# Attention and mixture of experts on one core: sums of squares in bfloat16, and the last scatter behind a branch

## The chip, the core and the metric

The kernel runs as one program on one core of a Trainium2 chip. Its time is the device time in microseconds (us) of one execution; where several runs were made, the median is given. The engines are named as the profile names them: PE is TensorE (PEld its weight loads), DVE is VectorE, ACT is ScalarE, POOL is GpSimd and SP is SyncE, which here issues most of the DMAs. A letter q behind a name (POOLq) marks instructions of the engine's sequencer: branches, semaphore waits, loads of a register.

## The reference

Attention of two kinds is added and goes, as 4608 rows of 512 numbers, into a mixture of eight experts, of which each row takes the likeliest one.

```python
# q, k, v: 8 batches x 8 heads x 576 x 64, float32
out_d = sm_attn(mean of 4 rows of q, of k, of v)        # 144 x 144, then repeated 4 times
mask = np.abs(pos[:, None] - pos[None, :]) < 4
attn = softmax(where(mask, 0.125 * q @ k.T, -1e9))
x = (repeat(out_d, 4) + attn @ v)                       # -> x: 4608 x 512

N, D, E, F = (4608, 512, 8, 1024)
logits = normed(x) @ normed(expert_emb).T / tau
expert_idx = np.argmax(logits, axis=1)
gate_w = softmax(logits)[arange(N), expert_idx]
for e in range(E):
    mask = expert_idx == e
    h = np.maximum(x[mask] @ w1[e], 0.0)                # 512 -> 1024
    out[mask] = gate_w[mask, None] * (h @ w2[e])        # 1024 -> 512
```

All inputs and the output are float32.

## The kernel before

**Stages.** Attention runs first (32 units of a batch and two heads, until about 335 us); its rows go to DRAM (`xd`) and are sorted by expert. The experts' part works in slots of 128 rows that all have one expert: an expert's rows are padded to whole slots, so their number depends on the data. Up to 43 + 3 slots are written out: 3 early ones, which take rows of the first six batches, 38 fixed ones (`NFIX`), which always run, and up to 5 further ones (`last_slots`), which stand in a branch on a flag (`flg`) that the routing writes. With these inputs the flag is zero: 41 slots run, and the further ones don't.

**One slot.** `gather` fetches 128 rows of x by an indirect DMA on POOL (L1091). They are split into two float16 parts and turned. `mm1` multiplies them by the expert's first weights, which lie as two float16 parts `w1h` and `w1l` too: 96 products of 128x128 by 128x128, three to each block (L1170 to L1172). ACT and DVE make the hidden rows from them (L1181, L1182), again as two parts `hT`. `mm2_part` of the slot before multiplies by the second weights, 24 products with 512 columns (L1193 to L1195). `out_rows` scales by the gate `gt` into a tile `o` of two buffers (ACT, L1202), and `store` scatters its 128 rows to their places in the output by an indirect DMA on POOL (L1206). `scale_gate` (POOL, L1157) makes `gt`.

**The weights' scale.** The float16 parts need a power of two near the weights' size. For it each weight matrix that arrives in `st` is squared and summed along its rows by ACT (`square`, L840) into a column of `wsq` (128x2: one column for the first weights, one for the second). In every fixed slot but the last, `total` adds `wsq` over the 128 partitions by a product with a matrix of ones (PE, L848), and DVE takes the result from the bank (L849); `scales` makes the scale and its inverse from the exponent (DVE, L856 and L858). `renew` then decides, by flags of the slot, whether the next slot has a new expert: if so, `split_all` splits the weights (ACT L864, DVE L865, in four pieces), if not, `measure` squares the next ones that have arrived. `measure_now`, in a branch of its own for weights that weren't measured in time, doesn't run with these inputs (no row of L992 in the trace).

**What sets the order.** The whole order is written by hand (`manual_schedule`): each engine's instructions stand in the program in the order in which the code issues them, and tiles with their number of buffers set the waits. Where `renew` branches, each engine concerned takes the branch for itself; the side that isn't taken ends with instructions that bring the semaphores to where the other side would have left them.

**The end.** After the last fixed slot come its second product, `out_rows` and `store`. Then `last_slots` loads the flag into a register on every engine (L1075), and every engine branches (L1076). Where the flag is zero, each engine brings its semaphores up; POOL does it for the eight semaphores of the software DMAs (those that POOL issues) too, with six semaphore instructions and one INC_SWDGE_SEM. Then the program ends (L1334): SP waits for all semaphores, every engine drains, and POOL clears the semaphores.

Of the kernel before, what the change touches and what calls it, by code (L numbers as in the profile page):

```python
# [8 lines left out]
F32 = mybir.dt.float32  # L9
F16 = mybir.dt.float16  # L10
BF16 = mybir.dt.bfloat16
I32 = mybir.dt.int32
AF = mybir.ActivationFunctionType
ALU = mybir.AluOpType
AX = mybir.AxisListType
# [5 lines left out]
N, DM, E, FF = B * S, H * D, 8, 1024  # L21
# [9 lines left out]
SLOT = 128  # L31
NSLOT = N // SLOT + E - 1
NEARLY, BEARLY = 3, B - 2
AHEAD = 4
NFIX = NSLOT - 5
# [14 lines left out]
class Kern:  # L50
# [761 lines left out]
    def weight_tiles(self):  # L812
        w = self.wp = self.pool(self.ctx, "weights", 1)
        self.w1h = w.tile([128, self.KC, FF], F16, name="w1h")
        self.w1l = w.tile([128, self.KC, FF], F16, name="w1l")
        self.w2h = w.tile([128, self.FC, DM], F16, name="w2h")
        self.w2l = w.tile([128, self.FC, DM], F16, name="w2l")
        self.wss = [w.tile([128, NP], F32, name=f"wss{j}") for j in range(2)]
        self.jk = w.tile([128, FF * self.KC // NP], BF16, name="junk")
        self.wmx = w.tile([128, 2], F32, name="wmx")  # L820
        self.wsq = w.tile([128, 2], F32, name="wsq")
        self.wk2 = w.tile([128, 2], I32, name="wk2")
        self.winv = w.tile([128, 2], F32, name="winv")
        self.wscl = w.tile([128, 2], F32, name="wscl")
        self.wold = w.tile([128, 1], F32, name="wold")
        self.wout = w.tile([128, 1], F32, name="wout")
# [6 lines left out]
        n, k = FF // 2, 2 * self.KC // NP  # L833
        return t[:, p % 2 * k:(p % 2 + 1) * k, p // 2 * n:(p // 2 + 1) * n]

    def square(self, src, which, p):

        junk = self.jk[:, :src.shape[1] * src.shape[2]].rearrange("p (c f) -> p c f", c=src.shape[1])
        acc = self.wsq[:, which:which + 1] if p is None else self.wss[which][:, p:p + 1]
        self.nc.scalar.activation(out=junk, in_=src, func=AF.Square, accum_out=acc)  # L840

    def pieces_sum(self, which):
        self.nc.vector.reduce_sum(out=self.wsq[:, which:which + 1], in_=self.wss[which], axis=AX.X)

    def total(self, c):

        ps = self.bank()[:, :c.stop - c.start]
        self.nc.tensor.matmul(out=ps, lhsT=self.onesf, rhs=self.wsq[:, c], start=True, stop=True)  # L848
        self.nc.vector.tensor_scalar(out=self.wmx[:, c], in0=ps, scalar1=1e-36, scalar2=None, op0=ALU.max)  # L849

    def scales(self, c):
# [21 lines left out]
    def first_weights(self):  # L873
# [25 lines left out]
        for p in range(NP):  # L899
            tiles.append(get(0, p))  # L900
            yield FREE
        yield LIGHT
        square(0, 0, 1)
        yield LIGHT
        square(0, 2, 3)
        yield FREE
        self.total(slice(0, 1))
# [9 lines left out]
        split(0, 3)  # L917
        yield LIGHT
        square(1, 0, 1)
        yield LIGHT  # L920
        square(1, 2, 3)
# [66 lines left out]
    def measure_now(self, which):  # L988

        g, c = self.nc.gpsimd, slice(which, which + 1)  # L990
        self.measure(which)
        g.partition_all_reduce(self.wmx[:, c], self.wsq[:, c], channels=128, reduce_op=bass.bass_isa.ReduceOp.add)  # L992
        g.tensor_scalar(out=self.wmx[:, c], in0=self.wmx[:, c], scalar1=1e-36, scalar2=None, op0=ALU.max)
        self.scales(c)

# [27 lines left out]
    def run_slots(self, q0, q1):  # L1023

        last = q1 - 1
        for q in range(q0, q1):
            b = q - NEARLY
            if b + 2 < q1 - NEARLY:
                self.flags(b + 2)
            if q + 2 < q1:  # L1030
                self.x_split(q + 2)
            self.mm1(q)
            if not b:
                self.mm2_part(q - 1, 6, ps=self.begun)
            if q < last:
                self.rescale()
                self.renew(0, b + 1)
                self.stage_next(0, b + 1)
            if not b:
                self.out_rows(q - 1, self.begun)  # L1040
                self.store(q - 1)
            if q + 4 < q1:
                self.gather(q + 4)
            if q < last:
                self.norms(q + 1)
            if q + 3 < q1:
                self.x_size(q + 3)
            self.logits(q)
            if q > q0:
                ps = self.mm2_part(q - 1)  # L1050
                if q < last:
                    self.out_rows(q - 1, ps)
            if q > q0:
                self.renew(1, b)
                if q == last:
                    self.out_rows(q - 1, ps)
                self.stage_next(1, b)
            self.gate(q)
            if q > q0:
                self.store(q - 1)  # L1060
            self.scale_gate(q)
        self.mm2(last)
        self.store(last)

    def open_slots(self, q):

# [131 lines left out]

    def out_rows(self, q, ps):
        s = self.sl[q]  # L1200
        o = s["o"] = self.mg.tile([SLOT, DM], F32, name="o", bufs=2)
        self.nc.scalar.activation(out=o, in_=ps, func=AF.Copy, scale=s["gt"])  # L1202

    def store(self, q):
# [5 lines left out]
    def run(self):  # L1210
        tc, ctx = self.tc, self.ctx
        ctx.enter_context(tc.manual_schedule())
        self.bk = self.pool(ctx, "banks", 7, space=PSUM)
        self.inv = self.pool(ctx, "inverses", 1, space=PSUM).tile([128, 2, G + 4], F32, name="inv")
        self.cp = self.pool(ctx, "const", 1)
        self.dr = self.pool(ctx, "scratch", 1, space=DRAM)
        self.weight_tiles()
        self.slot_pools()
        n = B * NHP
        with ExitStack() as actx:  # L1220
            w0 = self.first_weights()
            steps = self.attention(actx)
            early, heavy = self.early_slots(), FREE
            for at in steps:
                if at is None:
                    break
                if at in EARLY:
                    next(early)
                i, end = at
                if end and i >= 1 and i % NHP in heavy:  # L1230
                    heavy = next(w0, ())

            ps = self.begun
            self.x_size(2)
            self.mm1_half(0, 0, 2, 3, ps[0])
            next(steps)
            self.mm1_half(0, 0, 3, 4, ps[0])
            ps.append(self.mm1_half(0, 1, 0, 2))
            next(steps)
            next(steps)  # L1240
            for _ in steps:
                pass
        self.hd = self.pool(ctx, "hidden", 2)
        self.hidden(0, 0, ps[0])
        self.x_split(2)
        self.mm1_half(0, 1, 2, 4, ps[1])
        self.hidden(0, 1, ps[1])
        self.sw = self.pool(ctx, "slots", 1)
        slots = self.slots()
        next(slots)  # L1250
        w1 = self.second_weights()
        next(w1)
        self.norms(1)
        self.norms(2)
        for _ in range(2):
            next(w1)
        next(slots)
        self.mm1(1)
        ps = self.mm2_part(0, 0, 4)
        next(slots)  # L1260
        for q in range(AHEAD):
            self.gather(NEARLY + q)
        self.mm2_part(0, 4, ps=ps)
        for _ in range(2):
            next(w1)
        self.gates(0)
        self.out_rows(0, ps)
        flags = self.slot_flags()
        next(flags)
        next(slots)  # L1270
        self.hidden(2, 0, self.mm1_half(2, 0))
        self.store(0)
        self.x_T(NEARLY)
        self.hidden(2, 1, self.mm1_half(2, 1))
        next(flags)
        self.norms(NEARLY)
        for _ in range(4):
            next(w1)
        self.gates(1)
        ps = self.mm2_part(1)  # L1280
        next(slots)
        self.out_rows(1, ps)
        self.begun = self.mm2_part(2, 0, 6)
        self.store(1)
        self.x_T(NEARLY + 1)
        for _ in w1:
            pass
        self.gates(2)
        self.x_size(NEARLY + 2)
        self.flags(1)  # L1290
        self.run_slots(NEARLY, NEARLY + NFIX)
        self.last_slots()


@with_exitstack
# [42 lines left out]
```

## Time and profile before

| | |
|---|---|
| time, three runs | 758.92, 760.79 (median), 761.32 us |
| the profiled execution's own time | 763.65 us |
| its span, from the first to the last instruction | 761.9 us |
| PE busy | 715.3 us, 94% of the span |
| DVE, ACT, POOL busy | 464.5, 468.3, 398.8 us |
| attention, to 335 us: PE busy | 304.51 us |
| slots, 342 to 748 us | PE busy 403.7 of 406 us, granted clock 1.00 |
| from 748 us to the end | no matmul |

In a row of a group stand the line, the engine, the operation, output<-inputs, the shape and the count; then the busy time in us and the mean of one in ns; then the time for which the engine stood idle just before, and what ended it. In a row of a stretch each engine has its busy time and count, then come the granted TensorE clock (1.00 is full), the share of the DMA engines and their GB/s. A matmul's record is longer than the distance to the next one's start, since matmuls are pipelined.

### The profile page before, as it was taken

Reading aid. Unit: us, or ns where it says so; the run is one execution under the profiler, and the core shown is the slowest. Engines: PE = TensorE matmul, PEld = TensorE weight load, DVE = VectorE, ACT = ScalarE, POOL = GpSimd, SP = SyncE. Lnnn points to the kernel's source line nnn. Section 1 sums busy time; section 2 is a strip of 40 time slices with the busy share of each in tenths; the row PEclk is TensorE's granted clock in tenths of the full one; section 3 lists DMA queues with packets and bytes.
Section 4 is the critical chain, followed back from the end, with each engine's and each line's share of the span. In section 5 each row is a group of like instructions: output and inputs, shape, how many; then the busy total and the mean of one; then the engine's idle time right before and its main releaser. Section 6 shows DMA issues by size and latency. Waiting matters only on the chain. (4 is left out here: it accounts for less than half of the span.)

```text
span 761.9 us, 27560 instructions
## 1 busy us (share of the span) xinstructions
PE 715.3 (94%) x10540; PEld 542.1 (71%) x10540; DVE 464.5 (61%) x1395; ACT 468.3 (61%) x1095; POOL 398.8 (52%) x800
## 2 busy tenths in 40 slices
PE   7899799999988988999999999999999999999992
PEld 4678587777767767767776777677777777777760
DVE  6577578777778975866636656464654365456320
ACT  4577767778777844465755857676673367357420
POOL 7544455684586653737554555536455444535411
PEclk9999989989999967999999999999999999999997
DMA  9999999999999944735755637378584356338200
GB/s 164 162 206 211 186 205 163 247 160 236 175 198 201 152 162 100 211 78 164 183 98 166 185 113 239 80 213 155 175 181 86 84 155 174 85 125 199 61 27 19
DMA packets 191239, 117.82 MB, mean 155 GB/s; under 512 B 162898, under 2 KB 162898, under 8 KB 191072
## 3 DMA queue, kind: packets, MB, share of 16 engines
q1 hardware_dynamic: 183264, 94.61, 59.1%
q0 software_dynamic: 6560, 19.03, 7.9%
q10 hardware_dynamic: 1248, 2.11, 0.9%
q8 instruction: 85, 1.39, 0.8%
q14 instruction: 82, 0.67, 0.3%
HBM read 213.12 MB, written 20.33 MB: 306 GB/s over the span
## 5 line engine op out<-in xcount | busy, mean ns | idle before, releaser
L1172 PE MATMUL bank<-xT,w1l 128*128 128x128 f16 x1312 | 223.7, 220 | 1.9 <-DVEq L1013 0.8
L1171 PE MATMUL bank<-xT,w1h 128*128 128x128 f16 x1312 | 223.7, 220 | 0.3 <-issue 0.3
L1170 PE MATMUL bank<-xT,w1h 128*128 128x128 f16 x1312 | 223.7, 220 | 0.0
L1170 PEld LDWEIGHTS <-w1h 128*128 128x128 f16 x1312 | 128.8, 98 | 6.1 <-issue 2.0
L1171 PEld LDWEIGHTS <-w1h 128*128 128x128 f16 x1312 | 128.7, 98 | 4.3 <-issue 0.5
L1172 PEld LDWEIGHTS <-w1l 128*128 128x128 f16 x1312 | 128.8, 98 | 3.1 <-DVE w1l L865 2.0
L1195 PE MATMUL bank<-w2h,hT 128*128 128x512 f16 x328 | 124.3, 379 | 0.0
L1194 PE MATMUL bank<-w2l,hT 128*128 128x512 f16 x328 | 124.2, 379 | 0.0
L1193 PE MATMUL bank<-w2h,hT 128*128 128x512 f16 x328 | 124.2, 379 | 0.0
L1206 POOL DMA_INDIRECT out_dram<-o,ids x41 | 53.5, 1305 | 124.1 <-ACTq L1008 82.3
L1182 DVE SCALAR_TENSOR_TENSOR hT<-bank,hT 128x512 f16<-128x512 f32 x82 | 54.9, 686 | 46.0 <-ACT hT L1181 20.1
L390 POOL TENSOR_TENSOR pool_v<-ld_v 72x256 f32<-72x256 f32 x64 | 46.7, 750 | 64.2 <-DMA ld_v<-in_v_dram 48.9
L1181 ACT ACTIVATE hT<-bank 128x512 f16<-128x512 f32 x82 | 46.7, 587 | 52.7 <-PE bank L1172 38.3
L840 ACT ACTIVATE junk<-st 128x1024 bf16<-128x1024 f32 (+1 forms) x30 | 67.5, 2249 | 2.3 <-POOL at L602 1.5
L1121 DVE SCALAR_TENSOR_TENSOR x<-xg,sc,x 128x512 f16<-128x512 f32 x41 | 30.8, 751 | 60.7 <-ACT x L1118 55.2
L1091 POOL DMA_INDIRECT xg<-xd,ids x41 | 44.3, 1080 | 38.5 <-POOLq L1014 17.0
L381 POOL TENSOR_TENSOR pool_kq<-kq 128x288 f32<-128x288 f32 x62 | 43.6, 723 | 34.5 <-ACT kq L368 32.6
L472 ACT ACTIVATE aT<-bank 70x384 f32<-70x384 f32 x96 | 40.0, 484 | 34.0 <-PE bank L469 33.9
L1195 PEld LDWEIGHTS <-hT 128*128 128x128 f16 x328 | 32.0, 98 | 38.8
L1193 PEld LDWEIGHTS <-hT 128*128 128x128 f16 x328 | 35.0, 107 | 33.8
L1194 PEld LDWEIGHTS <-hT 128*128 128x128 f16 x328 | 32.0, 97 | 33.8
L1139 ACT ACTIVATE lg<-lg,lmx 128x8 f32<-128x8 f32 x41 | 12.3, 300 | 67.2 <-DVE lmx L1137 67.2
(236 smaller groups left out, 1547.6 us busy)
## 6 DMA issues: line engine op xcount, KB each, us to landing
st<-in_moe_w_dram SPq DMA_DIRECT2D x148, 1024.0 KB
ld_k<-in_k_dram SPq DMA_DIRECT2D x64, 144.0 KB
ld_q<-in_q_dram SPq DMA_DIRECT2D x64, 144.0 KB
ld_v<-in_v_dram SPq DMA_DIRECT2D x16, 576.0 KB
vw<-in_v_dram SPq DMA_DIRECT2D x16, 576.0 KB
xd<-xr SPq DMA_DIRECT2D x8, 1040.0 KB
st<-in_moe_w_dram SPq DMA_DIRECT2D x12, 512.0 KB
st<-in_moe_w_dram ACTq DMA_DIRECT2D x4, 512.0 KB
```

Of the source, the lines that this page charges most:

```text
L390: g.tensor_tensor(out=t6[:, h], in0=vr[:, :, 0:2 * D], in1=vr[:, :, 2 * D:], op=ALU.add)
L840: self.nc.scalar.activation(out=junk, in_=src, func=AF.Square, accum_out=acc)
L1091: nc.gpsimd.indirect_dma_start(out=xg, out_offset=None, in_=self.xd[:n], in_offset=bass.IndirectOffsetOnAxis(ap=self.ids[:, q:q + 1], axis=0),
L1170: nc.tensor.matmul(out=o, lhsT=self.w1h[:, k, f], rhs=xT[:, 0, k], start=(k == 0), stop=False)
L1171: nc.tensor.matmul(out=o, lhsT=self.w1h[:, k, f], rhs=xT[:, 1, k], start=False, stop=False)
L1172: nc.tensor.matmul(out=o, lhsT=self.w1l[:, k, f], rhs=xT[:, 0, k], start=False, stop=(k == self.KC - 1))
L1181: nc.scalar.activation(out=h[:, 0], in_=ps, func=AF.Relu)
L1182: nc.vector.scalar_tensor_tensor(out=h[:, 1], in0=ps, scalar=0.0, in1=h[:, 0], op0=ALU.max, op1=ALU.subtract)
L1193: nc.tensor.matmul(out=ps, lhsT=hh, rhs=self.w2h[:, j, :], start=(j == 0), stop=False)
L1194: nc.tensor.matmul(out=ps, lhsT=hh, rhs=self.w2l[:, j, :], start=False, stop=False)
L1195: nc.tensor.matmul(out=ps, lhsT=hl, rhs=self.w2h[:, j, :], start=False, stop=(j == self.FC - 1))
L1206: nc.gpsimd.indirect_dma_start(out=self.out, out_offset=bass.IndirectOffsetOnAxis(ap=self.ids[:, q:q + 1], axis=0), in_=o, in_offset=None, ...
```

## The change

There are two edits.

1. `wsq` is kept in bfloat16, and `total` multiplies it by bfloat16 ones (`onesb`, which the routing uses too) in place of float32 ones (`onesf`). `square` and `pieces_sum` write bfloat16; the sum that leads to it is still made in float32 by the engine that writes it. `measure_now` squares into a float32 tile of its own (`wsqf`), since POOL's sum over the partitions reads that, and copies it to `wsq`.
2. `run_slots` doesn't store its last slot any more, unless it is the last of the further ones. The last fixed slot's `store` is called behind `last_slots`, and its rows lie in a tile of their own, `oend`.

```diff
-        self.wsq = w.tile([128, 2], F32, name="wsq")
+        self.wsq = w.tile([128, 2], BF16, name="wsq")
+        self.wsqf = w.tile([128, 2], F32, name="wsqf")
...
-    def square(self, src, which, p):
+    def square(self, src, which, p, acc=None):
...
-        acc = self.wsq[:, which:which + 1] if p is None else self.wss[which][:, p:p + 1]
-        self.nc.scalar.activation(out=junk, in_=src, func=AF.Square, accum_out=acc)
+        if acc is None:
+            acc = self.wsq[:, which:which + 1] if p is None else self.wss[which][:, p:p + 1]
+        with self.nc.allow_low_precision(reason="an exponent is all that is taken of it"):
+            self.nc.scalar.activation(out=junk, in_=src, func=AF.Square, accum_out=acc)
...
     def total(self, c):
...
-        self.nc.tensor.matmul(out=ps, lhsT=self.onesf, rhs=self.wsq[:, c], start=True, stop=True)
+        self.nc.tensor.matmul(out=ps, lhsT=self.onesb, rhs=self.wsq[:, c], start=True, stop=True)
...
     def measure_now(self, which):
...
-        self.measure(which)
-        g.partition_all_reduce(self.wmx[:, c], self.wsq[:, c], channels=128, reduce_op=bass.bass_isa.ReduceOp.add)
+        self.square(self.st[which], which, None, self.wsqf[:, c])
+        self.nc.vector.tensor_copy(out=self.wsq[:, c], in_=self.wsqf[:, c])
+        g.partition_all_reduce(self.wmx[:, c], self.wsqf[:, c], channels=128, reduce_op=bass.bass_isa.ReduceOp.add)
...
     def run_slots(self, q0, q1):
...
-        self.store(last)
+        if q1 == NEARLY + NSLOT:
+            self.store(last)
...
     def out_rows(self, q, ps):
...
-        o = s["o"] = self.mg.tile([SLOT, DM], F32, name="o", bufs=2)
+        end = q == NEARLY + NFIX - 1
+        o = s["o"] = self.sw.tile([SLOT, DM], F32, name="oend") if end else self.mg.tile([SLOT, DM], F32, name="o", bufs=2)
...
     def run(self):
...
         self.last_slots()
+        self.store(NEARLY + NFIX - 1)
```

How the instructions stand on two engines follows; the line numbers of the changed kernel are a few higher. The first place is PE in a fixed slot, between the first product (L1172, with the turned rows `xT` and the weights `w1l`) and the second (L1193) of the slot before, with the total in the middle. Before:

```order
L1172 LDWEIGHTS w1l
L1172 MATMUL bank<-xT_6893,w1l 128x128
L848 MATMUL bank<-wsq,onesf 128x2
L1193 LDWEIGHTS hT
L1193 MATMUL bank<-w2h,hT 128x512
```

And now (L1178 and L1199 are the L1172 and L1193 of before):

```order
L1178 LDWEIGHTS w1l
L1178 MATMUL bank<-xT_6894,w1l 128x128
L852 LDWEIGHTS onesb
L852 MATMUL bank<-wsq,onesb 128x2
L1199 LDWEIGHTS hT
L1199 MATMUL bank<-w2h,hT 128x512
```

The total now has a weight load of its own in the order, with the bfloat16 ones, and stands at the same place between the same two products.

The second place is POOL's end: the scatters of the last two slots (`out_dram<-o,ids`, where `ids` are the places of the rows), the last `gt`, the flag, the branch, and behind it what the further slots would do. Before, the rows at the branch:

```order
L1206 DMA out_dram<-o,ids 4608x512
L1157 TENSOR_TENSOR gt<-gt,wout 128x1
L1206 DMA out_dram<-o,ids 4608x512
L1075 TENSOR_LOAD flg
L1076 COMPARE_AND_BRANCH
```

The last rows of POOL's program before:

```order
L1157 TENSOR_TENSOR gt<-gt,wout 128x1
L1206 DMA out_dram<-o,ids 4608x512
L1076 UNCONDITIONAL_BRANCH
L1076 ISA
L1076 UNCONDITIONAL_BRANCH
L1334 ISA
```

And now POOL's rows at the branch (L1097 is the first gather of the further slots):

```order
L1213 DMA out_dram<-o,ids 4608x512
L1163 TENSOR_TENSOR gt<-gt,wout 128x1
L1081 TENSOR_LOAD flg
L1082 COMPARE_AND_BRANCH
L1097 DMA xg<-xd,ids 128x520 x4
```

The last rows of POOL's program now:

```order
L1213 DMA out_dram<-o,ids 4608x512
L1163 TENSOR_TENSOR gt<-gt,wout 128x1
L1213 DMA out_dram<-o,ids 4608x512
L1082 UNCONDITIONAL_BRANCH
L1082 ISA
L1082 UNCONDITIONAL_BRANCH
L1213 DMA out_dram<-oend,ids 4608x512
L1342 UNCONDITIONAL_BRANCH
L1342 ISA
```

The last scatter has moved from ahead of the flag's load to behind the branch, where its rows come from `oend`; the scatters of `o` at the end of each list's second part are those of the further slots. On POOL it stands behind the INC_SWDGE_SEM (among the rows `ISA`) of the side that runs. The order of ACT, DVE and SP around it is as before.

More of the change, by code (lines that the diff above doesn't have):

```diff
@@ L834, in piece @@
         return t[:, p % 2 * k:(p % 2 + 1) * k, p // 2 * n:(p // 2 + 1) * n]
-    def square(self, src, which, p):
+    def square(self, src, which, p, acc=None):
         junk = self.jk[:, :src.shape[1] * src.shape[2]].rearrange("p (c f) -> p c f", c=src.shape[1])
-        acc = self.wsq[:, which:which + 1] if p is None else self.wss[which][:, p:p + 1]
-        self.nc.scalar.activation(out=junk, in_=src, func=AF.Square, accum_out=acc)
+        if acc is None:
+            acc = self.wsq[:, which:which + 1] if p is None else self.wss[which][:, p:p + 1]
+        with self.nc.allow_low_precision(reason="an exponent is all that is taken of it"):
+            self.nc.scalar.activation(out=junk, in_=src, func=AF.Square, accum_out=acc)
     def pieces_sum(self, which):
-        self.nc.vector.reduce_sum(out=self.wsq[:, which:which + 1], in_=self.wss[which], axis=AX.X)
+        with self.nc.allow_low_precision(reason="an exponent is all that is taken of it"):
+            self.nc.vector.reduce_sum(out=self.wsq[:, which:which + 1], in_=self.wss[which], axis=AX.X)
     def total(self, c):
         ps = self.bank()[:, :c.stop - c.start]
-        self.nc.tensor.matmul(out=ps, lhsT=self.onesf, rhs=self.wsq[:, c], start=True, stop=True)
+        self.nc.tensor.matmul(out=ps, lhsT=self.onesb, rhs=self.wsq[:, c], start=True, stop=True)
         self.nc.vector.tensor_scalar(out=self.wmx[:, c], in0=ps, scalar1=1e-36, scalar2=None, op0=ALU.max)
```

## The prediction

> **What bounds the kernel now.** I read the page's first lines, then a table of busy time by stage, then the groups of instructions by line, and last the stretch of the trace around each edited place. The page shows TensorE (PE) busy for nearly the whole span:
>
> ```profile
> PE 715.3 (94%) x10540; PEld 542.1 (71%) x10540; DVE 464.5 (61%) x1395; ACT 468.3 (61%) x1095; POOL 398.8 (52%) x800
> ```
>
> A share over the whole span hides the stages, so here is the table by stage: attention until about 335 us, the slots from 342 to 748, and what follows the last matmul.
>
> ```profile
> core 0: us, PE busy (x) PEld busy (x) DVE busy (x) ACT busy (x) POOL busy (x), PEclk, DMA share, GB/s
> 0.00:335.00 335.00, 304.51 (x5901) 241.62 (x5902) 248.00 (x723) 225.98 (x710) 197.10 (x319) 0.94 0.92 181
> 342.00:450.00 108.00, 107.07 (x1216) 78.52 (x1216) 60.52 (x186) 68.46 (x107) 61.76 (x140) 1.00 0.58 151
> ...
> 650.00:748.00 98.00, 97.44 (x1043) 68.64 (x1040) 41.43 (x136) 43.37 (x75) 40.11 (x103) 1.00 0.37 100
> 748.00:762.00 14.00, 0.00 (x0) 0.00 (x0) 0.00 (x0) 0.61 (x1) 1.00 (x1) 0.62 0.02 4
> ```
>
> In the slots PE is busy for 107.07 of 108 us and 97.44 of 98 us at a granted clock of 1.00, while no other engine reaches 69 us there: whatever shortens PE's row of instructions shortens the slots. Then come 14 us with no matmul, in which the engines have one copy and one scatter to do. The change touches one product per slot in the first stretch and the order of GpSimd's (POOL's) work in the second, so the forecast has two terms.
>
> **The product with ones.** Each of 37 slots issues one `total`. Its rows by line and shape, and three places where matmuls start (start, length of the first, engine, line):
>
> ```profile
> L848 PE MATMUL bank<-wsq,onesf 128*128 128x2 f32 x74 | 12.3, 236 | 0.0
> L848 PEld LDWEIGHTS bank<-wsq,onesf 128*128 128x128 f32 x78 | 12.1, 194 | 0.3
> 413.23 0.22 PE L1172 MATMUL bank<-xT,w1l 128*128 128x128 f16 x1
> 413.28 0.34 PE L848 MATMUL bank<-wsq,onesf 128*128 128x2 f32 x2
> 413.48 0.38 PE L1193 MATMUL bank<-w2h,hT 128*128 128x512 f16 x1
> ...
> 736.87 0.22 PE L1172 MATMUL bank<-xT,w1l 128*128 128x128 f16 x1
> 736.93 0.38 PE L1193 MATMUL bank<-w2h,hT 128*128 128x512 f16 x1
> ```
>
> The 74 records are 37 totals of two passes each (the four weight loads over 74 are two one-column totals in attention, which I cost at nothing: nothing there shows that they bind). A float32 product takes two weight loads of 194 ns and two multiplications. What counts is not the 236 ns of a record, which overlaps its neighbours, but the distance between the starts around it: with a total L1193 starts 0.25 us after the last L1172 (413.23 to 413.48), without one 0.06 us (736.87 to 736.93). So a total costs PE about 0.19 us now. At 37 slots that is 7.1 us, the most that this part can bring.
>
> What the bfloat16 product will cost has a near row: the routing's product with the same tile of bfloat16 ones.
>
> ```profile
> L642 PEld LDWEIGHTS <-onesb 128*128 128x128 bf16 x30 | 1.2, 96 | 0.0
> 117.47 0.27 PE L642 MATMUL bank<-oh,onesb 128*128 128x40 bf16 x5
> 117.60 0.31 PE L520 MATMUL bank<-ident,xT 128*128 128x128 f32 x1
> ```
>
> One weight load is 96 ns, and five multiplications of 8 to 40 columns start within 0.13 us, 25 ns apart. I take 25 ns for the new total, since that row has the same weights and as few columns. The distance L1172 to L1193 becomes 56 + 25 = 81 ns in place of 252 (the starts to the ns are 413.226 and 413.478): 0.171 us less per slot. The other end is that a weight load of 96 ns between two other loads isn't hidden: 0.06 + 0.10 = 0.16, a saving of 0.09 us per slot. The Trainium skill, "TensorE: Matmul & The Clock Gate", section "Back-to-back issue gap", says that in a stream of weight load and matmul pairs the distance is set by both and is about 81 ns at 128 columns. The trace has 55 to 60 ns for such pairs here, so I don't follow it; by the page's figure the new total would bring 0.115 us per slot in place of 0.171.
>
> Not every slot can use it. Where the expert changes, the weights are split on ACT and DVE, and PE waits for the result:
>
> ```profile
> L1172 PE MATMUL bank<-xT,w1l 128*128 128x128 f16 x1312 | 223.7, 220 | 1.9 <-DVEq L1013 0.8 <-DVE w1l L865 0.7 <-issue 0.2
> L1172 PEld LDWEIGHTS <-w1l 128*128 128x128 f16 x1312 | 128.8, 98 | 3.1 <-DVE w1l L865 2.0 <-DVEq L1013 0.9
> L865 DVE SCALAR_TENSOR_TENSOR w1l<-st,wscl,w1h 128x1024 f16<-128x1024 f32 x32 | 39.2, 1279 | 9.7 <-ACT w1h L864 9.7
> 489.17 0.60 ACT L1181 ACTIVATE hT<-bank 128x512 f16<-128x512 f32 x1 [2.08 <-PE bank L848]
> 489.80 0.69 DVE L1182 SCALAR_TENSOR_TENSOR hT<-bank,hT 128x512 f16<-128x512 f32 x1 [1.82 <-ACTq L1015]
> 490.41 0.15 DVE L849 TENSOR_SCALAR wmx<-bank 128x2 f32<-128x2 f32 x1
> ...
> 492.43 3.68 DVE L865 SCALAR_TENSOR_TENSOR w1l<-st,wscl,w1h 128x1024 f16<-128x1024 f32 x3 [1.39 <-ACT w1h L864]
> ```
>
> The 32 splits are 8 experts of four pieces, of which seven experts are switched to in the slots; there DVE's L849 takes the total only behind L1182 of the same slot, which follows ACT's L1181, which reads the bank of the first product (L1170 to L1172). I read the splits' start as tied to the end of that product, not to the total. If PE passes the total 0.17 us sooner, it waits 0.17 us longer for w1l. I leave out these seven and two slots at the beginning where the wait is put down to DVE's branch L1013: 37 − 9 = 28 slots, 28 × 0.171 = **4.8 us**. The bounds are 28 × 0.09 = 2.5 and 37 × 0.171 = 6.3.
>
> The sums now come from ACT's and DVE's writes of a bfloat16 `wsq`. I take no cost: each writes one column. The total's wait moves from ACT's semaphore to DVE's, because `measure_now` now ends on a DVE copy. These copies stand in branches that don't run, but the total can't start until DVE has passed them:
>
> ```profile
> L1008 DVEq COMPARE_BRANCH  x2: 47/51/55, 504.5 to 510.7; - x2
> L848 PE MATMUL bank<-wsq,onesf x4: 223/237/251, 499.9 to 510.7; 128*128 128x2 f32 x4
> ```
>
> These are 12 us that hold two totals; DVE passes the branch of one slot at 504.5, and the next total is at 510.7, 6 us later. So the new wait costs nothing as long as DVE isn't 6 us late. Behind the total PE has the 24 matmuls of the second product, so a late DVE would hold those.
>
> **The last scatter.** The rows after the last matmul, the sequencers' ones by line (count, least/median/greatest ns, first and last start):
>
> ```profile
> 743.41 0.99 POOL L1206 DMA_INDIRECT out_dram<-o,ids  x1 [9.21 <-ACT o L1202]
> 744.43 0.19 POOL L1157 TENSOR_TENSOR gt<-gt,wout 128x1 f32<-128x1 f32 x1
> 747.93 0.69 ACT L1202 ACTIVATE o<-bank,gt 128x512 f32<-128x512 f32 x1 [4.80 <-PE bank L1195]
> 748.89 1.00 POOL L1206 DMA_INDIRECT out_dram<-o,ids  x1 [4.27 <-ACT o L1202]
> ...
> L1075 POOLq TENSOR_LOAD <-flg x1: 299/299/299, 748.7 to 748.7; - x1
> L1076 POOLq COMPARE_BRANCH  x1: 45/45/45, 749.0 to 749.0; - x1
> L1076 POOLq EVENT_SEMAPHORE  x6: 17/30/43, 751.9 to 752.4; - x6
> L1076 POOLq INC_SWDGE_SEM  x1: 1828/1828/1828, 752.5 to 752.5; - x1
> L1334 SPq EVENT_SEMAPHORE  x14: 17/28/28, 754.2 to 761.9; - x14
> L1334 POOLq DRAIN  x3: 46/107/6772, 754.3 to 761.7; - x3
> DMA to landing us min/median/max: 3.2/3.2/3.2
> ```
>
> POOL's sequencer reads the flag, takes the branch at 749.0 and stands 2.9 us until the first semaphore instruction of the else-side at 751.9. Six of those take 0.5 us, one INC_SWDGE_SEM 1.83 us, and a DRAIN then lasts 6.77 us, from 754.3 to 761.1. The Trainium skill, "Runtime: NRT & Kernel Launch", section "Instruction fetch mechanics", says that a taken branch out of the two-page window waits for a fetch of its page. The 2.9 us agree with that, and I use them as they are.
>
> With the scatter behind the branch, POOL is free after gt at 744.62 and goes to the branch while PE still works. On the clock of before: flag 744.5, branch 744.8, else-side at 744.8 + 2.9 = 747.7, its semaphores to 748.2, INC to 750.04, and some 0.6 us for six waits that now stand ahead of the scatter (as long as the six of the else-side). The scatter then starts at 750.65, 1.76 us later than now; `oend` is long written (748.62). It ends at 751.65. If the DRAIN costs 6.77 us behind POOL's last work, as now, it ends at 758.4, and with the 0.85 us after it (761.1 to 761.95) the span ends at 759.25: **2.7 us sooner**. What the branch cost is hidden behind the last slot's matmuls. SP's final waits move to 751.65 − 1.0 + 3.2 = 753.85, and aren't late.
>
> What the DRAIN waits for isn't shown, since there is one long one in the trace. If it runs 8.6 us from the INC's start and the scatter goes beside it, it ends at 748.2 + 8.6 = 756.8: 4.2 sooner, or as much as 6.9 if the landing and SP's waits end it. If the scatter has to wait for that same work, it starts at 756.8, lands at 760.0, and the span ends at 760.9: 1.0 sooner. If the DRAIN's end hangs on the last scatter (748.89 to 761.1, 12.2 us), it ends at 762.85: 1.75 later. I take 2.7, because the DRAIN follows POOL's last instruction directly and no row shows work beside it.
>
> **Sum.** −4.8 in the slots and −2.7 at the end make −7.5 us. The profiled execution took 763.65 (span 761.9 and 1.75 around it), 2.9 above the median of 760.79, so it becomes 756.2 and the median 753.3. The rest that could move is attention's clock, 0.94 on average in its row; the three runs shown spread by 2.4 us.
>
> **Rivals.**
> - The DRAIN hangs on the last scatter: PE's 4.8 less 1.75, time 757.7. For it: the rows are scattered by software DMA, and the DRAIN is on the engine that issued it. Against: the scatter lands 3.2 us after its issue, long before 761.1. 0.14.
> - The scatter queues behind the work that the INC left: −4.8 − 1.0, time 755.0. 0.11.
> - That work runs beside the scatter: −4.8 − 4.2 to −6.9, time 751.8 to 749.1. 0.10.
> - The product's gain is lost, because the weight load isn't hidden or every slot has a wait to fill: the end's 2.7 alone to 2.5 + 2.7, time 758.1 to 755.6. Against: only 3.1 us of waits in all the slots' L1172. 0.07.
> - Slower: the total waits for DVE. It would need DVE to pass the branch L1008 over 6 us later than now in a slot; from there on each microsecond counts, and the change as a whole is lost at 7.5 us, 0.2 us in each of 37 slots. At 0.3 us it is 760.79 − 2.7 − 4.8 + 11.1 = 764.4. Against it stands the 6 us. 0.03.
>
> **How the numbers follow.** The likeliest case has 0.55 and gives **753.3**, by itself 752 to 754.6 (the slots between 4.8 − 1.2 and 6.3). The range for 8 in 10 is 750.0 to 757.6: it holds the likeliest, the two cases with the INC's work for the most part, most of a lost product gain, and the edge of the DRAIN that hangs on the scatter. About 0.3%, 2.3 us, is what a measurement of this kernel can tell from no change. Faster by more than that: 0.55 + 0.11 + 0.10, most of 0.14 (0.11) and half of 0.07, or 0.91 rounded up a little for the sizes; within it 0.06; slower 0.03.
>
> **What would show it.** In the changed trace L1172 to L1193's counterpart should be 0.08 us apart across the total, with one record per total, and the slots end about 4.8 us sooner. The waits for w1l should grow by about 1 us in all. POOL's flag load should come before the last matmul, its scatter within 3.6 us of it, and one DRAIN of about 6.8 us directly behind. A DRAIN of a different length, a scatter that starts at 12 us or more after the flag, or a total that waits for DVE would prove the sum wrong.

## The result, and the profile after

The changed kernel takes 738.14 us (median of four runs, 734.07 to 742.27), against 760.35 for the kernel before beside it: a ratio of 0.971 (95% interval 0.965 to 0.977). The forecast was 753.3, with a range down to 750.0. The gain is three times the one that was forecast, and the profile shows at once where the missing part is. The profiled execution took 736.54 us with a span of 734.5; here are page lines and three stretches of it:

```profile
PE 695.5 (95%) x10501; PEld 525.0 (71%) x10501; DVE 464.1 (63%) x1395; ACT 467.3 (64%) x1095; POOL 404.3 (55%) x800
PEclk8999999999999998999999999999999999999997
q1 hardware_dynamic: 183264, 94.61, 56.7%
L390 POOL TENSOR_TENSOR pool_v<-ld_v 72x256 f32<-72x256 f32 x64 | 45.2, 725 | 52.9 <-DMA ld_v<-in_v_dram 35.8
0.00:320.00 320.00, 295.99 (x5997) 236.90 (x5998) 249.49 (x735) 227.38 (x716) 196.28 (x319) 0.97 0.86 191
322.00:430.00 108.00, 105.77 (x1206) 76.84 (x1207) 60.90 (x186) 67.85 (x106) 62.64 (x140) 1.00 0.54 151
723.00:735.00 12.00, 0.54 (x3) 0.04 (x1) 0.00 (x0) 0.69 (x1) 1.00 (x1) 0.65 0.01 3
```

The same lines of before that weren't shown yet (the granted clock in forty slices, the queue of SP's loads, POOL's pooling of v, and the first 320 us):

```profile
PEclk9999989989999967999999999999999999999997
q1 hardware_dynamic: 183264, 94.61, 59.1%
L390 POOL TENSOR_TENSOR pool_v<-ld_v 72x256 f32<-72x256 f32 x64 | 46.7, 750 | 64.2 <-DMA ld_v<-in_v_dram 48.9
0.00:320.00 320.00, 290.02 (x5754) 232.38 (x5755) 236.61 (x685) 217.20 (x691) 188.15 (x305) 0.94 0.95 185
```

The slots now begin near 321 us in place of 342, with 243 more matmuls recorded in the first 320 us. The loads' queue moved the same 183264 packets and 94.61 MB in less time (59.1% of 761.9 us is 450 us on each of 16 engines, 56.7% of 734.5 is 416), and POOL waited 35.8 us for `ld_v` in place of 48.9. The profiled execution of before was slower than its kernel's median and that of the changed kernel faster than its own, so the profiles part by more (27.45 us) than the medians do (22.2). By the starts of matmuls they part as follows:

| stretch | before | after | difference | forecast |
|---|---|---|---|---|
| to the first total of the fixed slots | 341.64 | 320.79 | −20.85 | 0 |
| first to last total | 384.55 | 381.66 | −2.89 | −4.8 (with the next row) |
| last total to the last matmul's start | 20.88 | 20.71 | −0.17 | |
| last matmul's start to the end | 14.87 | 11.33 | −3.54 | −2.7 |
| span | 761.94 | 734.49 | −27.45 | −7.5 |

The changed kernel's attention varies from run to run: in another profiled execution its first total came at 327.2. The question was thus what two edits that aren't in attention take out of it: the work itself, or where they leave the other tiles. `wsqf` takes 32 bytes in each partition by the tiles' addresses in the program, and it stands ahead of nearly all tiles that are made later. The tiles `ld_k`, `ld_q` and `ld_v`, into which k, q and v are loaded, moved from 224 past a multiple of 256 bytes to a multiple of 256. The loads of k and q come in packets of 256 bytes, and so do those of the windows of v (`vw0`, `vw1`); those into `ld_v` are of 2048 bytes.

### The profile page after: what moved, and what is told of

It reads as the page before. It is cut to its first block, busy times and chain, and to the rows that moved or that the text cites. A ratio compares the mean times of both kernels' runs of the same rounds, so it can differ in the third digit from the quotient of the medians.

```text
span 734.5 us, 27477 instructions
## 1 busy us (share of the span) xinstructions
PE 695.5 (95%) x10501; PEld 525.0 (71%) x10501; DVE 464.1 (63%) x1395; ACT 467.3 (64%) x1095; POOL 404.3 (55%) x800
## 3 DMA queue, kind: packets, MB, share of 16 engines
q1 hardware_dynamic: 183264, 94.61, 56.7%
## 5 line engine op out<-in xcount | busy, mean ns | idle before, releaser
L1178 PE MATMUL bank<-xT,w1l 128*128 128x128 f16 x1312 | 223.2, 219 | 3.9 <-DVEq L1018 1.4
L1178 PEld LDWEIGHTS <-w1l 128*128 128x128 f16 x1312 | 128.6, 98 | 5.8 <-DVE w1l L869 2.5
L1199 PE MATMUL bank<-w2h,hT 128*128 128x512 f16 x328 | 124.2, 379 | 0.0
L1213 POOL DMA_INDIRECT out_dram<-o,ids x40 | 51.0, 1275 | 110.0 <-ACTq L1013 73.0
L1187 ACT ACTIVATE hT<-bank 128x512 f16<-128x512 f32 x82 | 46.6, 586 | 48.9 <-PE bank L852 34.4
L390 POOL TENSOR_TENSOR pool_v<-ld_v 72x256 f32<-72x256 f32 x64 | 45.2, 725 | 52.9 <-DMA ld_v<-in_v_dram 35.8
L1097 POOL DMA_INDIRECT xg<-xd,ids x41 | 44.3, 1081 | 39.4 <-POOLq L1019 17.6
L381 POOL TENSOR_TENSOR pool_kq<-kq 128x288 f32<-128x288 f32 x62 | 47.5, 787 | 30.6 <-ACT kq L368 28.7
L1201 PEld LDWEIGHTS <-hT 128*128 128x128 f16 x328 | 32.0, 98 | 38.7
L1199 PEld LDWEIGHTS <-hT 128*128 128x128 f16 x328 | 32.0, 98 | 33.8
L1200 PEld LDWEIGHTS <-hT 128*128 128x128 f16 x328 | 32.0, 98 | 33.8
```

What stands on the lines that cost most here:

```text
L381: g.tensor_tensor(out=t2[:, w], in0=k4[:, w, :, 0:2], in1=k4[:, w, :, 2:4], op=ALU.add)
L390: g.tensor_tensor(out=t6[:, h], in0=vr[:, :, 0:2 * D], in1=vr[:, :, 2 * D:], op=ALU.add)
L1178: nc.tensor.matmul(out=o, lhsT=self.w1l[:, k, f], rhs=xT[:, 0, k], start=False, stop=(k == self.KC - 1))
L1187: nc.scalar.activation(out=h[:, 0], in_=ps, func=AF.Relu)
L1199: nc.tensor.matmul(out=ps, lhsT=hh, rhs=self.w2h[:, j, :], start=(j == 0), stop=False)
L1200: nc.tensor.matmul(out=ps, lhsT=hh, rhs=self.w2l[:, j, :], start=False, stop=False)
```

## The experiments

**Four kernels that part the places from the edits.** `shift32` adds only this to the kernel before:

```diff
         self.wsq = w.tile([128, 2], F32, name="wsq")
+        self.wpad = w.tile([128, 2], F32, name="wpad")
```

> The kernel before with one unused tile of 128x2 float32 (32 bytes per partition) behind wsq, and nothing else, so that nearly every later tile lies 32 bytes higher, as in the changed kernel. Theory A (the places): the loads of q, k and v then land at multiples of 64 bytes, their 256-byte packets take 18 ns at the median in place of 22, attention ends near 320 us in place of 341, and the time is 737 to 746 us. Theory B (the work: the bfloat16 sums or the order of the engines took 21 us out of attention): nothing changes, 758 to 762 us, first product of the fixed slots at 341 us.

Measured: 745.35 us, ratio 0.982 (0.979 to 0.986), at the upper end of theory A's range. An unused tile alone took 14.7 us out, and theory B fell. In attention the median packet of 256 bytes took 18 ns, in the kernel before 22. In the profiled execution, the slowest of its six (751.95 us), the first total came at 330.1, not near 320.

`after_shift64` is the changed kernel with 32 bytes more, so that the tiles of loads lie 64 bytes higher than before:

```diff
         self.wsqf = w.tile([128, 2], F32, name="wsqf")
+        self.wpad = w.tile([128, 2], F32, name="wpad")
```

> The changed kernel with one unused tile of 32 bytes more, so that the later tiles lie 64 bytes higher than before: the loads of q, k and v are back at 32 past a multiple of 64. Both edits are in it. Theory A: 256-byte packets at 22 ns again, attention to about 341 us, and only the slots' 2.9 to 4.8 us and the end's 3.5 us are gained: 752 to 755 us. Theory B: as the changed kernel, 734 to 742 us.

Measured: 759.28 us, ratio 1.001 (0.998 to 1.004), above theory A's range by 4 us. Both edits are in it, and it isn't faster than before. The slots gained 2.6 us in its profile and the end 3.55, but neither theory had 759: its attention was longer than the edits account for, which the shift by 64 bytes below takes up.

`total_bf16` has the first edit alone (with the same 64 bytes), `store_last` the second alone:

> The bfloat16 sums and the total with bfloat16 ones alone, with the last scatter ahead of the branch as before, and tiles 64 bytes higher (loads of q, k and v at the same remainder as before). Theory A: the slots gain 0.168 us each where no wait takes it back, 2.9 to 4.8 us in all, the end nothing: 755.5 to 757.5 us. Theory B, if it is the total: 738 to 746 us.

> The moved scatter alone, with oend (2048 bytes, a multiple of 64) and the float32 total. Theory A: attention and slots as before; the stretch from the last matmul to the end is 11.3 us in place of 14.9: 756.9 us, between 755.5 and 758. Theory B, if the moved scatter or oend were what changed attention: 738 to 746 us.

Measured: `total_bf16` 761.29 us, ratio 1.003 (1.000 to 1.006): a miss of 4 us. Its profile has the slots 3.6 us shorter, but the first total at 346.6, 4.9 later than before. `store_last` 756.68 us, ratio 0.995 (0.992 to 0.998), with the stretch after the last matmul at 11.47 us: as expected of theory A.

**Which places.** The next kernels only move tiles. `shift64` and `shift96` are `shift32` with 64 and 96 bytes; `attention32` puts the 32 bytes ahead of attention's tiles alone; `after_vw` is the changed kernel with pads among attention's tiles, which move `vw0` and `vw1` and others of that pool (its `kq`, `xT`, `an` and `sums`) too:

```diff
+        self.apad = self.pool(ctx, "apad", 1).tile([128, 8], F32, name="apad")     # attention32
         self.ld = self.pool(ctx, "ld", 2)
...
         for i in range(2):
+            self.zpad = z.tile([128, (16, 40)[i]], F32, name=f"zpad{i}")           # after_vw
```

> The kernel before with unused tiles of 64 bytes per partition behind wsq, float32 total and the scatter ahead of the branch. The loads of q, k and v are at 32 past a multiple of 64 again, as before, but 64 bytes further on. Theory A (only the remainder to 64 counts): as before, 758 to 762 us, 256-byte packets at a mean of 26.8 ns. Theory A2 (the remainder to 256 counts, 224 before and 32 here): 763 to 767 us with packets at 28 ns, since the two kernels with this shift and with the bfloat16 total had an attention about 5 us longer than the edits account for. Theory C (the bfloat16 sums make attention 5 us longer, whatever the places): 758 to 762 us too, and then the 5 us stay with the bfloat16 sums.

> The kernel before with 96 bytes per partition behind wsq: the loads of q, k and v are at multiples of 64 that are no multiples of 128 or 256. Theory A (a multiple of 64 is enough): like the shift by 32 bytes, 744 to 748 us, packets at 22.7 ns. Theory A2 (256 counts): between, 750 to 760 us.

> The kernel before with an unused tile of 32 bytes ahead of attention's tiles alone: the loads of q, k and v and the other attention tiles lie as in the shift by 32 bytes, the tiles of the slots (gathered rows, turned rows, staged weights) as before. Theory A: all of the gain is in attention's loads, 744 to 748 us. Rival: it comes from the staged weights or the slots' tiles, 758 to 762 us.

> The changed kernel with unused tiles of 64 and 160 bytes among attention's tiles, so that both tiles of windows of v (vw), which take packets of 256 bytes too, begin at multiples of 256; in the changed kernel one lies at 192 past and the other at 32 past one. Theory A: the half of the vw loads that lies at 32 past gets 4 ns a packet faster, attention shortens by some 1 to 5 us: 733 to 737 us. Rival: these loads are hidden, as the changed kernel, 738 us.

Measured, beside the kernel before at 763.86 us: `shift64` 768.92 us, ratio 1.006 (1.003 to 1.009), so 64 bytes do cost about 5 us, with the first total at 346.4 as in `total_bf16` (346.6): theory A in its first form (the remainder to 64) and theory C fell. The kernel before is 3 to 4 us slower beside these runs than beside the others, so the ratios count more than the ranges in us here: by its own time `shift64` is above theory A2's range, and `attention32` above theory A's. `shift96` 754.67 us, 0.989 (0.985 to 0.992): part of the gain, as theory A2 has it; `vw0` is at a multiple of 256 in it, so the gain isn't the multiple of 64 alone. `attention32` 751.43 us, 0.985 (0.980 to 0.990), which overlaps the 0.982 of `shift32`: the tiles of the slots have no part that shows. `after_vw` 736.65 us, 0.964 (0.960 to 0.968), which doesn't part its two theories yet.

**The loads alone.** `loads_only` moves the three tiles of loads by 32 bytes; all others keep their remainder to 512:

```diff
+        self.apad = self.pool(ctx, "apad", 1).tile([128, 8], F32, name="apad")
         self.ld = self.pool(ctx, "ld", 2)
+        self.apad2 = self.pool(ctx, "apad2", 1).tile([128, 120], F32, name="apad2")
```

> The kernel before with 32 unused bytes ahead of the tiles of the loads of q, k and v (ld_k, ld_q, ld_v) and 480 behind them, so that these three begin at multiples of 256 and every other tile keeps its remainder to 512; float32 total, scatter ahead of the branch. Theory A (the packets of these loads): most of the gain of the shift by 32 bytes, attention shorter by 8 to 17 us, ratio to the kernel before 0.98 to 0.99, at least 0.7 of the 256-byte packets at 18 ns in place of 0.53. Rival (tiles that the engines compute in): ratio 0.997 to 1.003, share 0.53.

Measured: 745.09 us, ratio 0.979 (0.976 to 0.982), all of what `shift32` had. The queue of loads and POOL's wait for `ld_v` in its profile:

```profile
q1 hardware_dynamic: 183264, 94.61, 53.9%
L392 POOL TENSOR_TENSOR pool_v<-ld_v 72x256 f32<-72x256 f32 x64 | 45.2, 727 | 26.9 <-DMA ld_v<-in_v_dram 25.6
0.00:320.00 320.00, 295.18 (x5973) 235.82 (x5974) 250.54 (x734) 226.22 (x714) 196.14 (x319) 0.97 0.83 191
```

And in that of `shift64`, on the other side:

```profile
q1 hardware_dynamic: 183264, 94.61, 60.3%
L390 POOL TENSOR_TENSOR pool_v<-ld_v 72x256 f32<-72x256 f32 x64 | 47.9, 768 | 70.5 <-DMA ld_v<-in_v_dram 66.2
0.00:320.00 320.00, 288.90 (x5689) 230.81 (x5690) 232.12 (x669) 217.04 (x688) 184.98 (x298) 0.91 0.97 184
```

The same packets and bytes, 66.2 against 25.6 us of waits for `ld_v`, and a granted clock of 0.91 against 0.97: only the places differ. Each trace has 155936 packets of 256 bytes: 73728 of k and q and 40224 of the windows of v in attention, and 41984 with which the slots turn x by DMA. The latter take 18 ns or less in 0.81 to 0.83 of the cases, whatever the kernel. The next table has the share at 18 ns or less of all these packets, and then of the packets into each place. For the latter, packets were matched with SP's loads in order of time and the middle three quarters of each load taken, so these are estimates:

| kernel | `ld_k`, `ld_q`, `ld_v` past 256 | `vw0`, `vw1` past 256 | share, all | share, k and q | share, `vw0`, `vw1` | time of q1 on each engine, us | first total at, us |
|---|---|---|---|---|---|---|---|
| `shift64` | 32 | 224, 64 | 0.51 | 0.49 | 0.14, 0.20 | 463 | 346.4 |
| before | 224 | 160, 0 | 0.53 | 0.47 | 0.14, 0.36 | 450 | 341.6 |
| `shift96` | 64 | 0, 96 | 0.56 | 0.52 | 0.40, 0.23 | 442 | 332.0 |
| `shift32` | 0 | 192, 32 | 0.77 | 0.94 | 0.48, 0.37 | 415 | 330.1 |
| after | 0 | 192, 32 | 0.77 | 0.94 | 0.50, 0.36 | 416 | 320.8 |
| `loads_only` | 0 | 160, 0 | 0.81 | 0.94 | 0.48, 0.68 | 400 | 322.6 |
| `after_vw` | 0 | 0, 0 | 0.83 | 0.94 | 0.72, 0.68 | 401 | 322.1 |

(The time of q1 is its share by the page times the span. The first total is that of one execution each; the changed kernel had 320.8 in one and 327.2 in another.) A packet of k or q takes 18.4 ns on average at a multiple of 256, 23.6 at 64 past it, and 24.5 at 32 and at 224 past it. At 73728 packets on 16 engines, the 6.1 ns between 24.5 and 18.4 are some 28 us of each engine's time. 128 past a multiple wasn't tried. That POOL waits less for `ld_v`, whose packets are of another size, is argued from the queue that it shares with k and q; no run moves `ld_v` alone.

The Trainium skill, "DMA: Bandwidth & Descriptors", section "How a descriptor splits into AXI transactions", says that a transaction must start at a multiple of 256 bytes, and that a descriptor which starts off that grid fetches the bytes from the boundary below it too, which cost beats (of 32 bytes). It speaks of bytes that are read, and not of the place in SBUF at which a packet lands. Taken for that place too, it agrees with the runs in that the multiple of 256 is the good one. The sizes don't follow its beats: estimated by its rule, a 256-byte packet at 32 past takes 8 + 1 beats and one at 224 past 8 + 7, and k and q took 24.5 ns at both. That `shift64` is slower than before goes with `vw1`, which left the multiple of 256 (0.36 to 0.20), more than with k and q.

**The end, and the better version.** `no_further` is the changed kernel without the call of `last_slots`. `after_again` is the changed kernel and `after_vw_again` the one with both `vw` tiles at multiples of 256, on one chip:

> The changed kernel without the branch for further slots (no flag, no branch, no INC_SWDGE_SEM; with other inputs rows would be missing). It prices the end. Theory M1 (a drain of 6.77 us behind POOL's last work): the scatter starts 1.8 us after the last matmul's start, ends at 2.8, and the drain and the close bring the end to 10.4 us after it, in place of 11.3: 0.9 us faster than the changed kernel. Theory M2 (the long drain is work that the INC leaves): the drain is under 0.2 us, and the end is set by the scatter's landing and SP's waits, 5.5 to 6.5 us after the last matmul: 5 to 6 us faster.

> The changed kernel again, beside the others of this call. All theories: ratio to the kernel before 0.965 to 0.977, 0.77 of the 256-byte packets at 18 ns.

> The changed kernel with both vw tiles at multiples of 256 again, on the same chip as the changed kernel. Theory A: 1 to 5 us faster than it (0.83 of the 256-byte packets at 18 ns in place of 0.77). Rival (the vw loads are hidden): the same within 1 us.

Measured: `no_further` 740.19 us, 0.972 (0.968 to 0.975); `after_again` 739.93, 0.972 (0.969 to 0.974); `after_vw_again` 735.10, 0.965 (0.962 to 0.968). So moving the windows of v gives 4.8 us more, with intervals that don't overlap, and that version beats both kernels. The share of `vw0` and `vw1` at 18 ns rose from 0.50 and 0.36 to 0.72 and 0.68, so these loads aren't hidden, unless the 4.8 us come from the other tiles of their pool, which moved too; that isn't tested. `no_further` isn't faster than the changed kernel by the median, which varies by more than the 0.9 us in question; in its profile the end comes 10.03 us after the last matmul's start, where theory M1 had 10.4. Its trace settles what the drain isn't. Last matmul, scatter and drain of it are

```profile
729.77 0.38 PE L1201 MATMUL bank<-w2h,hT 128*128 128x512 f16 x1
731.21 1.00 POOL L1213 DMA_INDIRECT out_dram<-oend,ids  x1 [3.88 <-ACT oend L1209]
L1341 POOLq DRAIN  x3: 46/108/8012, 731.0 to 739.5; - x3
```

There is no INC_SWDGE_SEM in it, and the drain lasts until 731.0 + 8.0 = 739.0, 6.8 us behind the scatter's end at 732.2. M2 fell: the long drain isn't work that the INC leaves.

## Why the prediction was wrong

**The step that failed** is the one that gave attention no term: "I take no cost: each writes one column", "so the forecast has two terms", and "The rest that could move is attention's clock". The first edit brings a tile, and I costed its writes but not its place. By medians, 32 unused bytes alone took 14.7 us out (`shift32`), and the places of the three tiles of loads alone 15.6 (`loads_only`), of the 22.2 us that were gained. In the profiled executions 20.85 of 27.45 us lie ahead of the first total; by the changed kernel's other execution, whose first total came at 327.2, it is 14.4. The row that could have warned me was on the page of before: POOL waiting 48.9 us for `ld_v`, and a DMA share of 0.92 over attention. I had read attention as a stage that the change doesn't touch. None of my rivals had a mechanism in it.

How the faster loads become some 15 us is shown in part only: fewer waits (`ld_v`: 48.9 to 25.6 us in `loads_only`) and a higher granted clock (0.94 to 0.97) come together, and no run here parts the one from the other.

**The product with ones** was right as a price. Row and starts after:

```profile
L852 PE MATMUL bank<-wsq,onesb 128*128 128x2 bf16 x37 | 6.2, 167 | 0.0
L852 PEld LDWEIGHTS <-onesb 128*128 128x128 bf16 x39 | 3.8, 98 | 0.3
393.00 0.22 PE L1178 MATMUL bank<-xT,w1l 128*128 128x128 f16 x1
393.06 0.17 PE L852 MATMUL bank<-wsq,onesb 128*128 128x2 bf16 x1
393.09 0.38 PE L1199 MATMUL bank<-w2h,hT 128*128 128x512 f16 x1
```

One record per total, and 84 to 85 ns from the last product to L1199 (393.00 to 393.09) where I had 81 and the kernel before 251 to 252: 0.167 us a slot. It came in full in 21 of the 36 periods between totals. No total waited for DVE: its row has 0.0 us of idle time ahead.

**The waits that take it back** were undersized: nine slots without the full gain became fifteen of the 36 periods. Five of the seven slots with a switch gave nothing, as forecast (the other two lost a wait of 0.3 us that `shift32` and `store_last` lost too, so it isn't the total's). The first period is 0.55 us longer, and that isn't the total's either: `shift32` has the same. But PE now also meets a wait in each second slot behind a switch, seven in all, at 0.05 to 0.75 us each; in the kernel before, only the first of these slots was longer than its neighbours (10.87 us in place of 10.73). The dearest one, by its matmuls and DVE's branches:

```profile
L1178 PE MATMUL bank<-xT,w1l 128*128 128x128 f16 x1312 | 223.2, 219 | 3.9 <-DVEq L1018 1.4 <-DVE w1l L869 1.3 <-DVEq L1019 1.1
354.87 0.22 PE L1177 MATMUL bank<-xT,w1h 128*128 128x128 f16 x1
355.74 0.23 PE L1178 MATMUL bank<-xT,w1l 128*128 128x128 f16 x1 [0.66 <-DVEq L1019]
...
L1018 DVEq COMPARE_BRANCH  x1: 50/50/50, 355.2 to 355.2; - x1
L1019 DVEq EVENT_SEMAPHORE  x1: 21/21/21, 355.7 to 355.7; - x1
```

L1178 reads w1l, which DVE may rewrite in the branch, so it must wait until DVE has passed it, which is at 355.7. DVE is late there: w2's splits of the switch held it from 346.5 to 351.4, and the rest of the slot's work stood behind them (that this is the whole cause is argued from the order of its rows). The waits ahead of L1178 rose from 1.9 to 3.9 us. From the first to the last total the gain was 2.9 us in place of 4.8; in the six other profiles with this edit it was 2.5 to 3.9, since the size of these waits differs from one execution to the next.

**The end** had the right mechanism and one wrong start. POOL's rows and SP's:

```profile
719.50 0.99 POOL L1213 DMA_INDIRECT out_dram<-o,ids  x1 [9.21 <-ACT o L1209]
720.52 0.19 POOL L1163 TENSOR_TENSOR gt<-gt,wout 128x1 f32<-128x1 f32 x1
723.16 0.38 PE L1201 MATMUL bank<-w2h,hT 128*128 128x512 f16 x1
725.88 1.00 POOL L1213 DMA_INDIRECT out_dram<-oend,ids  x1 [5.17 <-issue]
L1081 POOLq TENSOR_LOAD <-flg x1: 296/296/296, 719.3 to 719.3; - x1
L1082 POOLq COMPARE_BRANCH  x1: 45/45/45, 719.6 to 719.6; - x1
L1082 POOLq EVENT_SEMAPHORE  x6: 17/30/43, 722.2 to 722.7; - x6
L1082 POOLq INC_SWDGE_SEM  x1: 1800/1800/1800, 722.8 to 722.8; - x1
L1342 POOLq DRAIN  x3: 46/113/8002, 725.7 to 734.2; - x3
L1342 SPq EVENT_SEMAPHORE  x14: 17/28/3941, 724.5 to 734.4; - x14
```

The drain ends at 733.65 (725.65 + 8.00), 6.77 us behind the scatter's end at 726.88: the time that the INC's end and the drain's had between them before (754.3 to 761.1). By the traces' unrounded times it ends 6.78 to 6.80 us behind POOL's last piece of work in all fourteen profiles, be that the INC (seven) or the scatter (seven); the rivals in which it hangs on the INC, or on the scatter's issue 12.2 us before, fell. What it waits for in this time no run shows. The scatter starts 2.72 us after the last matmul's start where I had 3.58 (750.65 − 747.07). I had let POOL read the flag after `gt`; its sequencer read it at 719.3, ahead of the scatter and of `gt` that stand before it in the order (in the rows of before it did so too: the flag at 748.7, the scatter at 748.89). So the branch was begun 1.3 us sooner, by the last matmul's start, than I had it, and it took 2.6 us (719.6 to 722.2) in place of 2.9. The scatter gave 0.7 us of that back: it starts 1.3 us behind the INC's end (724.56 to 725.88), where I had 0.6. What is left, 0.86 us, is what the end gained beyond the forecast (3.54 and 2.7).

So by the edits' own merits the forecast of −7.5 us was near (−6.6 in the profile without attention), in part by luck: the slots gave 1.7 us less than I had and the end 0.8 more. By medians at equal places the edits bring some 4 us (`after_shift64` beside `shift64`) to 9 (the changed kernel beside `shift32`), estimated from ratios to the kernel before that were not taken side by side. The time was still out of the range, by what the edits do to the places of others.

## What to carry to other kernels

A new tile can have a price, or a gain, even where nobody uses it: it moves the tiles that are made after it. Where a stage waits for loads of 256-byte packets, look up where their tiles begin, before the change and after it, and put them at multiples of 256 bytes (the best place of those tried here); to judge an edit, compare it with the kernel before at equal places. And where a stage's time moves that the edit doesn't touch, pad one tile before explaining the edit.

## What the runs showed of the hardware that I hadn't expected

- The 256-byte packets of k and q take 18 ns or less in 0.94 of the cases into tiles at a multiple of 256 bytes (18.4 ns on average), and in 0.47 to 0.52 at 32, 64 and 224 past one (23.6 to 24.5 ns).
- POOL's DRAIN at the program's end lasts until 6.8 us behind its last scatter or INC_SWDGE_SEM, whichever is later, and the rows of the scatter have long landed by then (2.5 us from issue in the changed kernel).
- POOL's sequencer ran ahead of its engine: it loaded the flag 0.2 us before the scatter and 1.3 us before the `gt` that stand ahead of the load.
